# Attention, experts and a gated second stage on one core: weight sums earlier, token splits staggered, a third load buffer, conversions moved

## The chip, the cores and the metric

The kernel runs on one core of one Trainium2 chip. The metric is device microseconds (us) for one execution, compared as medians of several runs. Five engines work side by side and meet by semaphores: TensorE (PE; PEld is its weight load), VectorE (DVE), ScalarE (ACT), GpSimd (POOL) and SyncE (SP), which here issues nearly all DMAs. Each engine takes its instructions strictly in the order in which they were written for it.

## The reference, cut to what matters

```python
x = attention(q, k, v)                       # 4 batches, 8 heads, 768 positions, 64 wide
x = x.reshape(3072, 512)
x = x + gate * (relu(x @ w1[e]) @ w2[e])     # for kept tokens; e = best of 8 experts; w1 512x1024, w2 1024x512
gate = 1 / (1 + exp(-(x @ w_gate)))          # second stage: w_gate, w_val 512x1536
val = x @ w_val
return (gate * val) @ w_out                  # w_out 1536x512
```

The inputs of the second stage's weights come as 8-byte floats, which the kernel turns into 4-byte ones itself.

## The kernel before, in words

**Order.** Attention with the routing comes first (to about 290 us), then the experts 1 to 7 (290 to 493 us) and one tile of overflow tokens (493 to 508 us), then the second stage (508 us to the end).

**Experts.** Each expert takes 256 tokens. Its first products are four groups (`hook1` is called after each), its second products four more (`hook2`). `hook2` splits the next expert's w1 into a high and a low part, one of four chunks at a call (`split_chunk`: ACT copies the high part, L798; DVE subtracts, L799). Both hooks also advance the conversions of the second stage's weights: `CSE[e]` says how many half conversions each of the eight calls makes. One conversion is a load by SP (`cv_load`, tile `cvw`, 512 KB), a square on ACT (L1359), five DVE operations (L1372 to L1379), an addition on POOL (L1380), and a store from ACT's queue (`cv_store`). 28 of the 36 conversions (`NCE`) are made in the experts, eight in the second stage, two half ones in each of its first steps. Loads run two conversions ahead in the experts and one ahead in the second stage.

**Second stage.** Tokens come in three groups of 1024, and each group makes twelve steps. A step (`first_product`) is a 2x2 matrix product in the form with seven products instead of eight. One side needs seven combinations of the four token blocks (`xsplit`, tiles `B11`, `B21`, `B22`, `B1` to `B4`), the other the four weight blocks and four sums of them (`wsums`, tile `ws`, four POOL additions, L1140 to L1143). Every operand is split into a high and a low part; a product is six matmuls of 128x512 (L1222). `wsplit(s, 0)` splits the weights themselves, `wsplit(s, 1)` the sums (L1149 on ACT, L1150 on DVE). DVE adds the products up (L1228); a step ends in sigmoids or in gate times value, and half of the hidden values go to DRAM (`hd`) and come back later.

**Items.** The output product is cut into items of 12 matmuls each (L1189). An item's weights are loaded four items ahead (`item_load`, tile `wo`, with `hf` for the hidden values that come back), and split two items ahead (`item_split`: ACT L1171 and L1178, DVE or POOL L1172, DVE L1179). From step 2 on, each step carries one item in between its products. After the twelfth step of the first and the second group, twelve items run alone, and among them lies the change to the next group's tokens: at the third and the seventh of the twelve, PE turns the tokens of one half (`turn`, L1095) into the four banks of PSUM that the products use too, and `xsplit` works through them, one piece after each quarter of an item. `xsplit` for half 0 subtracts the low parts of its combinations on POOL, for half 1 on DVE (L1107).

**Entry to the second stage.** SP issues `load_w(0)`, `load_w(1)` and the token loads at the end of the experts. The order written out at the start of the second stage is: `wsums(0)` on POOL, both `wsplit` of step 0, `load_w(2)`, `wsums(1)`, both turns, both `xsplit` interleaved, loads and splits of the first items, then the steps. There are four banks for turned tokens and products together (`ps_a`), so a product needs the bank of a piece that `xsplit` has read for the last time.

Of the kernel before, what the change touches and what calls it, by code (L numbers as in the profile page):

```python
# [9 lines left out]
F32 = mybir.dt.float32  # L10
F32R = mybir.dt.float32r
I32 = mybir.dt.int32
U32 = mybir.dt.uint32
AF = mybir.ActivationFunctionType
ALU = mybir.AluOpType
# [3 lines left out]
P = 128  # L19
# [4 lines left out]
DM = H * D  # L24
# [28 lines left out]
NSTEP = NGR * NM  # L53
# [2 lines left out]
FAR = BIG * 2.0 ** H  # L56
WT1, WT2, WT3 = 2, 3, 3
NCE = 28
C7 = 1, 1, 1, 1, 1, 1, 1, 2
CSE = (None, (0, 0, 1, 1, 0, 1, 1, 1), C7, C7, C7, C7, C7, (1, 1, 1, 1, 1, 1, 0, 0))  # L60


def _i32(c):
# [4 lines left out]
def attention_moe_glu_kernel(  # L68
# [7 lines left out]
    nc = tc.nc  # L76
    n_global, n_local, g_gate, g_val, g_out = [a.bitcast(I32) for a in (n_global, n_local, g_gate, g_val, g_out)]
    cp = ctx.enter_context(tc.tile_pool(name="cp", bufs=1))
# [40 lines left out]
    raw_p = wctx.enter_context(tc.tile_pool(name="raw_p", bufs=2))  # L119
# [637 lines left out]
    def cv_load(n):  # L757
        if n < 3 * NM:
            cvw[n] = load_words(nc, cvp, f"g{n}", cv_src(n)[0])
# [4 lines left out]
        wr = cvw.pop(n)  # L764
        return convert(nc, cvp, f"g{n}", wr, squares(nc, cvp, f"g{n}", wr), cvt[n])

    wf = {}

    def load_w(s):
        if s < NSTEP:  # L770
            wf[s] = cvp.tile([P, 4, 2 * P], F32, tag="w", name=f"w{s}")
            nc.sync.dma_start(wf[s], wd[s % NM].rearrange("p m c f -> p m (c f)").rearrange(
                "p m (k e) -> p (m k) e", k=2))

    def cv_store(n):
        if n in cvt:
# [3 lines left out]
    with ExitStack() as ectx:  # L780
# [254 lines left out]
        run(conv)  # L1035
        load_w(0)
        load_w(1)

        x0 = [cvp.tile([P, 2, DM], F32, tag="cvw", name=f"xr0_{a}", bufs=4) for a in range(4)]

# [17 lines left out]
    with ExitStack() as gctx:  # L1058
# [12 lines left out]
        def tmp(tag, name, bufs=2):  # L1071
            return tm_p.tile([P, HT], F32, tag=tag, name=name, bufs=bufs)
# [27 lines left out]
        def xsplit(g, c, pt):  # L1100

            Bt = xB[g]

            def parts(k, src, eng):
                th = Bt[k][:, 0, c]
                A.activation(th, src, AF.Copy)  # L1106
                eng.tensor_tensor(Bt[k][:, 1, c], src, th.bitcast(F32), ALU.subtract)  # L1107

            E = (G, V)[c]
            tags = [("cp", 6)] * 5 if g == 0 and c else [("sg", 5)] * 5  # L1110
            t = [tmp(tag, f"t{g}_{c}_{k}", n) for k, (tag, n) in enumerate(tags)]
            A.activation(t[4], pt[0, 1], AF.Copy)
            parts("11", pt[0, 0], V)
            yield
            parts("21", pt[1, 0], V)
            yield
            V.tensor_tensor(t[0], t[4], pt[0, 0], ALU.subtract)
            yield
            V.tensor_tensor(t[1], pt[1, 1], t[0], ALU.subtract)  # L1119
            parts("2", t[1], E)  # L1120
            yield
            parts("1", t[0], E)
            yield
            V.tensor_tensor(t[2], pt[1, 1], t[4], ALU.subtract)  # L1124
            parts("3", t[2], E)
            yield
            V.tensor_tensor(t[3], pt[1, 0], t[1], ALU.subtract)
            parts("4", t[3], E)
            yield
            parts("22", pt[1, 1], V)  # L1130
            yield


        ws, wsp = {}, {}

        def wsums(s):
            if s < NSTEP:
                w = wf[s]
                t = ws[s] = tm_p.tile([P, 4, 2 * P], F32, tag="ws", name=f"ws{s}", bufs=1)
                G.tensor_tensor(t[:, 0], w[:, 2], w[:, 3], ALU.add)  # L1140
                G.tensor_tensor(t[:, 1], t[:, 0], w[:, 0], ALU.subtract)
                G.tensor_tensor(t[:, 2], w[:, 0], w[:, 2], ALU.subtract)
                G.tensor_tensor(t[:, 3], w[:, 1], t[:, 1], ALU.subtract)  # L1143

        def wsplit(s, i):
            if s < NSTEP:
# [10 lines left out]
        def item_load(n):  # L1157
            if n < len(items):
                g, h, m = items[n]
                wof[n] = tmp("wo", f"wo{n}")  # L1160
                nc.sync.dma_start(wof[n], od[m])
                if h:
                    hf[n] = tmp("hf", f"hf{n}")
                    nc.sync.dma_start(hf[n], hd[m])

        def item_split(n):
            if n < len(items):
                g, h, m = items[n]
                t = wos[n] = (tm_p if n % 3 == 2 else raw_p).tile([P, 2, DM], F32R, tag="raw", name=f"wos{n}", bufs=1 if n % 3 == 2 else 2)
                src = wof.pop(n)  # L1170
                A.activation(t[:, 0], src, AF.Copy)  # L1171
                (V if h else G).tensor_tensor(t[:, 1], src, t[:, 0].bitcast(F32), ALU.subtract)  # L1172
                if h:
                    hidden_split(g, h, m, hf.pop(n))
# [98 lines left out]

        def conversions():
            for n in range(NCE, 3 * NM):
                if n == NCE:
                    cv_load(n)
                cv_load(n + 1)
                it = cv_steps(n)
                next(it)  # L1280
                yield
                next(it)
                cv_store(n - 1)
                yield
            cv_store(3 * NM - 1)
# [1 line left out]
        conv = conversions()  # L1287


        wsums(0)  # L1290
        wsplit(0, 0)
        wsplit(0, 1)
        load_w(2)
# [8 lines left out]
        for n in range(4):  # L1302
            if n > 1:
                item_split(n - 2)
            item_load(n)
        n = 0
        for s in range(NSTEP):
            g, pk = divmod(s, NM)
# [508 lines left out]
```

## Time and profile before

| | us |
|---|---|
| median of 3 runs (lowest, highest) | 1125.66 (1125.36, 1126.01) |
| the profiled execution's own time | 1127.95 |
| its span, first to last instruction | 1126.2 |
| PE busy in the span | 1050.3 (93%) |
| DVE busy in the span | 832.0 (74%) |

The span is what the rows divide up. PE is busy nearly throughout, so the places to look for are those where PE waits, and what released it there; the timeline names the releaser in brackets behind an instruction.

### The profile page before, as it was taken

The numbers are of one execution on the slowest core, as the hardware profiler recorded it, in microseconds if no ns is written. First come the engines' busy times: TensorE is split into PE (matmuls) and PEld (weight loads), VectorE is DVE, ScalarE is ACT, GpSimd is POOL, SyncE is SP. The second block draws the span as 40 slices with busy tenths as digits, with TensorE's granted clock in tenths as the row PEclk, the third lists the DMA queues.
The fourth block names the chain that finished last, engine by engine and source line by source line (L and its number), as shares of the span: only waits on it lengthen the run. The fifth ranks groups of instructions, "written<-read, shape, count | busy, mean of one in ns | idle before, by whom it ended". The sixth has DMA issues, their size and how long they took to land. (4 is left out here: it accounts for less than half of the span.)

```text
span 1126.2 us, 16867 instructions
## 1 busy us (share of the span) xinstructions
PE 1050.3 (93%) x5602; PEld 853.4 (76%) x5602; DVE 832.0 (74%) x1693; ACT 531.1 (47%) x963; POOL 487.9 (43%) x523
## 2 busy tenths in 40 slices
PE   7999999998999898995698999989999989999998
PEld 7999999886776675754566678778888868888886
DVE  6778888874666878846688887757777775877653
ACT  5897878751333333334233334444344454343333
POOL 6665656551324343335355564114555311555410
PEclk8999999988999999997899999999999999999999
DMA  9565555523988888841333343533224444323144
GB/s 176 123 167 130 134 128 135 161 68 97 381 298 289 307 292 313 307 162 57 111 131 131 113 159 103 180 101 134 81 78 166 138 143 117 107 85 95 65 150 150
DMA packets 156387, 176.37 MB, mean 157 GB/s; under 512 B 84224, under 2 KB 106496, under 8 KB 156288
## 3 DMA queue, kind: packets, MB, share of 16 engines
q1 hardware_dynamic: 148384, 156.81, 45.1%
q10 hardware_dynamic: 5184, 9.44, 2.2%
q0 software_dynamic: 2720, 8.92, 2.1%
q8 instruction: 48, 0.79, 0.3%
q14 instruction: 51, 0.42, 0.1%
HBM read 133.45 MB, written 36.18 MB: 151 GB/s over the span
## 5 line engine op out<-in xcount | busy, mean ns | idle before, releaser
L1222 PE MATMUL p<-B,wsp 128*128 128x512 f32 x1512 | 373.4, 397 | 29.7 <-DVE cp L1228 14.7
L1222 PEld LDWEIGHTS p<-B,wsp 128*128 128x128 f32 x1512 | 286.3, 191 | 100.8 <-issue 24.1
L1189 PE MATMUL o<-wos,gt 128*128 128x512 f32 x864 | 220.6, 395 | 11.5 <-ACT gt L1178 7.4
L1228 DVE TENSOR_TENSOR cp<-p,cp 128x512 f32<-128x512 f32 x252 | 167.6, 684 | 75.3 <-PE p L1222 69.4
L1189 PEld LDWEIGHTS o<-wos,gt 128*128 128x128 f32 x864 | 162.3, 189 | 51.1 <-ACT gt L1178 9.7
L1172 POOL TENSOR_TENSOR wos<-wo,wos 128x512 fp32r<-128x512 f32 x36 | 61.3, 1704 | 110.1 <-ACT wos L1171 110.1
L401 ACT ACTIVATE p<-t,mn 128x256 f32<-128x256 f32 (+1 forms) x192 | 83.6, 485 | 38.7 <-DVE mn L392 38.1
L857 PE MATMUL y<-raw,hT 128*128 128x512 f32 x224 | 99.6, 592 | 0.0
L1235 ACT ACTIVATE sg<-cp 128x512 f32<-128x512 f32 x72 | 45.1, 632 | 114.9 <-DVE cp L1228 114.3
L1178 ACT ACTIVATE gt<-gm 128x512 fp32r<-128x512 f32 x36 | 22.8, 632 | 155.4 <-DVE gm L1242 155.4
L838 PE MATMUL h<-xeh,we 128*128 128x256 f32 x448 | 88.3, 297 | 7.5 <-DVE we L799 7.5
L1140 POOL TENSOR_TENSOR ws<-w 128x256 f32<-128x256 f32 x36 | 26.5, 737 | 153.3 <-DVE wsp L1150 144.8
L1380 POOL TENSOR_TENSOR cvd<-cvd,cvbg 128x512 f32<-128x512 f32 x36 | 58.1, 1620 | 64.3 <-issue 35.6
L392 DVE CUSTOM_DVE_ANT_0 t<-s,far 128x256 f32<-128x256 f32 (+1 forms) x192 | 69.0, 397 | 19.7 <-PE s L367 15.8
L279 POOL TENSOR_TENSOR ks<-ring,ks 128x384 fp32r<-128x384 f32 x56 | 56.2, 1024 | 60.6 <-DVE ks L278 52.3
L838 PEld LDWEIGHTS h<-xeh,we 128*128 128x128 f32 x448 | 72.7, 198 | 10.1 <-DVE we L799 8.2
L367 PE MATMUL s<-ks,qs 128*128 128x256 f32 (+1 forms) x384 | 70.5, 303 | 5.3 <-POOL ks L279 2.7
L857 PEld LDWEIGHTS y<-raw,hT 128*128 128x128 f32 x224 | 41.0, 190 | 43.6 <-issue 43.3
L439 PE MATMUL o<-v,pts 128*128 128x65 f32 x384 | 70.6, 276 | 0.0
L1238 POOL TENSOR_TENSOR gm<-cp,sg 128x512 f32<-128x512 f32 x36 | 53.4, 1483 | 30.3 <-DVE cp L1228 30.3
L838 PE MATMUL h<-xel,we 128*128 128x256 f32 x224 | 64.7, 289 | 0.0
L1150 DVE TENSOR_TENSOR wsp<-w,wsp 128x1024 fp32r<-128x1024 f32 x36 | 58.8, 1632 | 7.2 <-ACT wsp L1149 6.7
(276 smaller groups left out, 1932.4 us busy)
## 6 DMA issues: line engine op xcount, KB each, us to landing
raw<-in_moe_w_dram SPq DMA_DIRECT2D x68, 512.0 KB
w<-wd SPq DMA_DIRECT2D x36, 512.0 KB
wo<-od SPq DMA_DIRECT2D x72, 256.0 KB
hd<-gm SPq DMA_DIRECT2D x36, 256.0 KB
hf<-hd SPq DMA_DIRECT2D x36, 256.0 KB
qraw<-in_q_dram SPq DMA_DIRECT2D x32, 192.0 KB
kraw<-in_k_dram SPq DMA_DIRECT2D x32, 192.0 KB
v<-in_v_dram SPq DMA_DIRECT2D x8, 768.0 KB
```

The source lines that it names most:

```text
L367: nc.tensor.matmul(st[:, a, c0:256], qt[:, a, i * P:(i + 1) * P], kt[:, a, e, k0:(i + 1) * P], start=(e == 0), stop=(e == 1))
L392: nc.vector.tensor_tensor_reduce(o, i0, i1, 2.0 ** -(h0 + 1), 3.0e38, ALU.add, ALU.min, mn[:, a:a + 1])
L401: nc.scalar.activation(p[:, a, c0:], t[:, a, c0:], AF.Exp, bias=mn[:, a:a + 1], scale=-1.0)
L439: nc.tensor.matmul(o[:, hh, :], t[:, a, 1, :], vt[:, hh, i, :], start=(i == 0), stop=True)
L838: nc.tensor.matmul(ph[:, a, :n], chunks[cb + c][:, wl, m * P:(m + 1) * P], xx[:, c, :n], start=(s_ == 0), stop=(s_ == len(seq) - 1))
L857: nc.tensor.matmul(ys[u], hh[:, f % 2, u * P:(u + 1) * P], w[:, (f % 2) * DM:(f % 2 + 1) * DM], start=(f == 0), stop=(f == NF - 1))
L1150: V.tensor_tensor(t[:, 1], src, t[:, 0].bitcast(F32), ALU.subtract)
L1172: (V if h else G).tensor_tensor(t[:, 1], src, t[:, 0].bitcast(F32), ALU.subtract)
L1189: nc.tensor.matmul(o[u], gt[:, hl, u * P:(u + 1) * P], w[:, wl, :], start=(m == 0 and i == 0), stop=(m == NM - 1 and i == 2))
L1222: nc.tensor.matmul(ps, w[:, wl, q, c * P:(c + 1) * P], Bt[k][:, xl, c], start=i == 0, stop=i == len(seq) - 1)
L1228: V.tensor_tensor(into, ps, t, ALU.add)
L1380: nc.gpsimd.tensor_tensor(dst, dst, b, ALU.add)
```

## The change

Four things change. The four POOL additions of `wsums(0)` are written at the end of the experts' stage (tile `ws` moves to a pool that lives there). `xsplit` makes the same operations in five pieces instead of eight, with the low parts a piece behind the high ones, and the four differences sooner. `wo` and `hf` have three buffers instead of two (a third `raw` tile is taken from another pool for it). The conversions are counted out anew: more of an expert's half conversions after its first products, fewer among its second ones, none in the last expert's second products; in the second stage the first two loads are issued ahead of the steps, and later ones two ahead.

```diff
-C7 = 1, 1, 1, 1, 1, 1, 1, 2
-CSE = (None, (0, 0, 1, 1, 0, 1, 1, 1), C7, C7, C7, C7, C7, (1, 1, 1, 1, 1, 1, 0, 0))
+C7 = 2, 2, 1, 1, 0, 1, 1, 1
+CSE = (None, (0, 0, 1, 1, 0, 1, 1, 1), C7, C7, C7, C7, C7, (2, 2, 1, 1, 0, 0, 0, 0))
...
         load_w(0)
         load_w(1)
+        wsums(0)
...
             E = (G, V)[c]
+            src = {"11": pt[0, 0], "21": pt[1, 0], "22": pt[1, 1], "1": t[0], "2": t[1], "3": t[2], "4": t[3]}
+            sub = lambda o, x, y: V.tensor_tensor(o, x, y, ALU.subtract)
+            high("11")
             A.activation(t[4], pt[0, 1], AF.Copy)
-            parts("11", pt[0, 0], V)
+            high("21")
+            low(V, "11")
+            sub(t[0], t[4], pt[0, 0])
             yield
-            parts("21", pt[1, 0], V)
+            sub(t[1], pt[1, 1], t[0])
+            low(V, "21")
+            high("22")
             yield
-            V.tensor_tensor(t[0], t[4], pt[0, 0], ALU.subtract)
+            high("2", "1")
+            sub(t[2], pt[1, 1], t[4])
+            sub(t[3], pt[1, 0], t[1])
             yield
-            V.tensor_tensor(t[1], pt[1, 1], t[0], ALU.subtract)
-            parts("2", t[1], E)
+            low(E, "2", "1")
+            high("3", "4")
+            low(V, "22")
             yield
-            parts("1", t[0], E)
+            low(E, "3", "4")
             yield
-            ... (t[2], "3"; t[3], "4"; "22": three more pieces)
...
-                wof[n] = tmp("wo", f"wo{n}")
+                wof[n] = tmp("wo", f"wo{n}", 3)
...
-                    hf[n] = tmp("hf", f"hf{n}")
+                    hf[n] = tmp("hf", f"hf{n}", 3)
...
-                if n == NCE:
-                    cv_load(n)
-                cv_load(n + 1)
+                cv_load(n + 2)
...
-        wsums(0)
         wsplit(0, 0)
         wsplit(0, 1)
...
             item_load(n)
+        cv_load(NCE)
+        cv_load(NCE + 1)
```

(`parts` was the copy of a high part on ACT followed at once by the subtraction of the low part.)

## Rows read from the trace of the kernel before

**Rows 1.** Windows: length, busy us (x instructions) by engine, PE clock, DMA share, GB/s.
```profile
290.00:508.00 218.00, 210.05 (x1036) 144.98 (x1035) 157.72 (x220) 72.33 (x105) 82.50 (x60) 0.98 0.81 290
508.00:545.00 37.00, 18.92 (x76) 13.97 (x77) 23.15 (x29) 15.68 (x25) 15.75 (x15) 0.77 0.28 93
...
698.00:744.00 46.00, 40.46 (x181) 31.73 (x180) 34.04 (x47) 23.70 (x43) 9.17 (x7) 0.96 0.47 155
744.00:891.00 147.00, 147.00 (x650) 121.66 (x649) 106.60 (x132) 59.12 (x85) 69.82 (x71) 1.00 0.33 110
891.00:935.00 44.00, 38.53 (x176) 29.96 (x176) 32.23 (x46) 23.32 (x43) 8.45 (x6) 1.00 0.49 157
```
**Rows 2.** Timeline of PE, entry to second stage: start, us, count [idle before <-releaser].
```profile
508.72 3.69 PE L1095 MATMUL gx<-ident,xr 128*128 128x128 f32 x32 [1.10 <-DVEq L1735]
...
528.52 2.90 PE L1222 MATMUL p<-B,wsp 128*128 128x512 f32 x6 [6.63 <-DVE t L1127]
...
544.25 11.88 PE L1222 MATMUL p<-B,wsp 128*128 128x512 f32 x42 [6.82 <-DVE cp L1228]
```
**Rows 3.** Timelines of POOL, ACT, DVE and SP at the same entry.
```profile
508.69 2.02 POOL L912 DMA_INDIRECT x_rows<-xo,idx  x1 [12.04 <-DVEq L1735]
...
501.52 1.06 ACT L1149 ACTIVATE wsp<-w 128x1024 fp32r<-128x1024 f32 x1 [0.41 <-ACTq L1735]
513.67 1.06 ACT L1149 ACTIVATE wsp<-ws 128x1024 fp32r<-128x1024 f32 x1 [11.09 <-POOL ws L1143]
...
508.64 1.23 DVE L1150 TENSOR_TENSOR wsp<-w,wsp 128x1024 fp32r<-128x1024 f32 x1 [0.23 <-DVEq L1735]
515.90 2.69 DVE L1107 TENSOR_TENSOR B<-gx,B 128x512 fp32r<-128x512 f32 x4
...
541.54 0.43 DVE L1372 TENSOR_SCALAR cvd<-cvwg 128x512 int32<-128x512 int32 x1 [6.10 <-DMA cvwg<-in_moe_w_out_dram]
...
514.34 19.77 SPq L1161 DMA_DIRECT2D wo<-od  x4
...
535.28 0.86 SPq L1352 DMA_DIRECT2D cvwg<-in_moe_w_out_dram  x2
```
**Rows 4.** Groups by line, 508 to 545 us: xcount | busy us, mean ns | idle.
```profile
L1107 POOL TENSOR_TENSOR B<-t,B 128x512 fp32r<-128x512 f32 x4 | 5.5, 1386 | 5.9 <-ACT B L1106 5.9
L1107 DVE TENSOR_TENSOR B<-t,B 128x512 fp32r<-128x512 f32 x4 | 5.5, 1388 | 2.1 <-ACT B L1106 2.1
...
L1107 DVE TENSOR_TENSOR B<-gx,B 128x512 fp32r<-128x512 f32 x6 | 3.8, 682 | 0.1
```
**Rows 5.** Timeline of PE and DVE at the two changes of group.
```profile
716.18 2.60 PE L1189 MATMUL o<-wos,gt 128*128 128x512 f32 x10 [1.18 <-DVE gt L1179]
...
720.28 8.93 PE L1189 MATMUL o<-wos,gt 128*128 128x512 f32 x36
730.17 3.45 PE L1189 MATMUL o<-wos,gt 128*128 128x512 f32 x12 [0.96 <-ACT gt L1178]
736.44 7.42 PE L1189 MATMUL o<-wos,gt 128*128 128x512 f32 x24 [2.82 <-ACT gt L1178]
...
928.75 6.29 PE L1189 MATMUL o<-wos,gt 128*128 128x512 f32 x24 [2.80 <-ACT gt L1178]
...
714.37 1.75 DVE L1179 TENSOR_TENSOR gt<-hf,gt 128x512 fp32r<-128x512 f32 x1
```
**Rows 6.** Waits of SP, 676 to 746 us: total us, times, longest.
```profile
SPq L1161 <- DVE wos L1172: 23.9, 10, 5.4
```
**Rows 7.** The chain of waits at the first change of group: start, us.
```profile
720.58 2.79 DMA wo<-od
```
**Rows 8.** Waits, 280 to 510 us: total us, times, longest.
```profile
PE h L838 <- DVE we L799: 7.5, 3, 3.5
```
**Rows 9.** Timelines of SP and DVE inside the third expert.
```profile
355.86 2.04 SPq L1350 DMA_DIRECT2D cvwg<-in_moe_w_gate_dram  x2
...
367.18 1.89 DVE L1372 TENSOR_SCALAR cvd<-cvwg 128x512 int32<-128x512 int32 x1 [4.90 <-DMA cvwg<-in_moe_w_gate_dram]
```

More of the change, by code (lines that the diff above doesn't have):

```diff
@@ L765, in cv_steps @@
         return convert(nc, cvp, f"g{n}", wr, squares(nc, cvp, f"g{n}", wr), cvt[n])
-    wf = {}
+    wf, ws = {}, {}
     def load_w(s):
@@ L773, in load_w, with wsums @@
                 "p m (k e) -> p (m k) e", k=2))
+    def wsums(s):
+        if s < NSTEP:
+            w = wf[s]
+            t = ws[s] = cvp.tile([P, 4, 2 * P], F32, tag="ws", name=f"ws{s}", bufs=1)
+            for k, (x, y, op) in enumerate(((w[:, 2], w[:, 3], ALU.add), (t[:, 0], w[:, 0], ALU.subtract),
+                                            (w[:, 0], w[:, 2], ALU.subtract), (w[:, 1], t[:, 1], ALU.subtract))):
+                nc.gpsimd.tensor_tensor(t[:, k], x, y, op)
     def cv_store(n):
@@ L1102, in xsplit, with high, low @@
             Bt = xB[g]
[L1104 to L1107, printed above, removed]
+            tag, n = ("cp", 6) if g == 0 and c else ("sg", 5)
+            t = [tmp(tag, f"t{g}_{c}_{k}", n) for k in range(5)]
+            def high(*keys):
+                for k in keys:
+                    A.activation(Bt[k][:, 0, c], src[k], AF.Copy)
+            def low(eng, *keys):
+                for k in keys:
+                    eng.tensor_tensor(Bt[k][:, 1, c], src[k], Bt[k][:, 0, c].bitcast(F32), ALU.subtract)
@@ L1109, in xsplit @@
             E = (G, V)[c]
-            tags = [("cp", 6)] * 5 if g == 0 and c else [("sg", 5)] * 5
-            t = [tmp(tag, f"t{g}_{c}_{k}", n) for k, (tag, n) in enumerate(tags)]
+            src = {"11": pt[0, 0], "21": pt[1, 0], "22": pt[1, 1], "1": t[0], "2": t[1], "3": t[2], "4": t[3]}
+            sub = lambda o, x, y: V.tensor_tensor(o, x, y, ALU.subtract)
+            high("11")
             A.activation(t[4], pt[0, 1], AF.Copy)
-            parts("11", pt[0, 0], V)
+            high("21")
@@ L1121, in xsplit @@
+            high("3", "4")
+            low(V, "22")
             yield
-            parts("1", t[0], E)
+            low(E, "3", "4")
             yield
[L1124 to L1143, printed above, removed]
+        wsp = {}
@@ L1168, in item_split @@
                 g, h, m = items[n]
-                t = wos[n] = (tm_p if n % 3 == 2 else raw_p).tile([P, 2, DM], F32R, tag="raw", name=f"wos{n}", bufs=1 if n % 3 == 2 else 2)
+                t = wos[n] = xa.tile([P, 2, DM], F32R, tag="xT", name=f"wos{n}") if n % 3 == 2 else raw_p.tile([P, 2, DM], F32R, tag="raw", name=f"wos{n}")
                 src = wof.pop(n)
```

## The prediction, made before the changed kernel ran

> **What bounds the kernel now.** I read the windows by stage first. From 744 to 891 us PE is busy all 147.00 us with 650 instructions at full clock: 0.226 us a matmul, nothing to win there. The reader is to see the other stretches beside it: 508 to 545 us, where PE is busy 18.92 of 37.00 us and its granted clock averages 0.77 (between its two levels, 1.2 and 2.4 GHz), and the two changes of group, 698 to 744 and 891 to 935 us [rows 1]. At 0.226 us a matmul and 3.69/32 = 0.115 us a transposition, the change from 698 needs 149 x 0.226 + 32 x 0.115 = 37.4 us and takes 46.0, an excess of 8.6; the one from 891 needs 144 x 0.226 + 3.7 = 36.2 and takes 44.0, an excess of 7.8 [rows 1, 2]. Then the timelines say what PE waited for: in the entry 6.63 us for DVE's differences of tokens and 6.82 us for a DVE addition [rows 2], at the changes three kinds of waits for split operands [rows 5]. In the experts the waits of PE for DVE's weight splits come to 7.5 us [rows 8]. So PE sets the end, and what can be won is its waiting: about 18 us in the entry, 16 in the changes, 7.5 in the experts.
>
> **Part 1, the entry (weight sums, stagger, early conversion loads): 13 us.** Before, POOL stood idle 12.04 us, issued a scatter at 508.69 (2.02 us) and only then made the four sums, until 513.67: 2.96 us of work. ACT stood for 11.09 us on them, and behind it in ACT's order stood the first copies of tokens; DVE began the token split at 515.90 [rows 3]. Written ahead, the sums lie in POOL's 12.04 us. Their wait is for the weights' load, which was there when ACT copied the same weights at 501.52; behind them on POOL stands only that scatter. Without that cover they would cost 2.96 us again. DVE then goes on from 508.64 + 1.23 with the second weight split, another 1.2: done at 511.1, 4.8 us ahead of 515.90.
>
> What is late next is DVE's own work: per half seven operations on PSUM, in all 14 at 2.69/4 = 0.67 us, 9.4 us [rows 3], and four low parts of half 1 at 0.69 to 1.39 us, 2.8 to 5.6 us; the 2.1 us that it waited for ACT's copies are gone, for a copy now has a piece's time to finish (the lower end by the PSUM row, 0.68) [rows 4]. It ends at 523.3 to 526.1. Four high and low pairs of half 0 on POOL change their order and not their number.
>
> Then the conversion. DVE's first one stood 6.10 us, to 541.54, for a load that SP issued at 535.28, since SP was held until 514.34 + 19.77 = 534.1 by the third and fourth `wo` loads, which waited for the two buffers [rows 3]. Now the third has its own buffer. The fourth waits for the first item's split on POOL, which comes after the second sums (511.1 + 2.96 = 514.1) and four low parts at 1.39, so to about 520, and as much again for the split: 521.4. The conversion loads go out at about 522; issue to use was 541.54 - 535.28 = 6.26 us, so they land at 528.3. DVE gets there at 526 to 529 (an addition, a weight split, an addition: 0.68 + 1.23 + 0.68 = 2.6 us after the token split). PE went on 544.25 - 541.54 = 2.7 us after the conversion's start [rows 2, 3]: now 531.0 to 531.8. PE itself: seven products from about 512.4; at 2.7 us each, twice 6 x 0.226, as at the half clock (528.52: 2.90 for six), 18.9 us, also 531. Three chains end together, so I take 531.2 for 544.25: 13 us. Bounds: 4.8 (only the sums' lead counts, the load stays as late against DVE), and 15 (DVE at 523.3 + 2.6 + 2.7 = 528.6, the load in time). The eight steps that follow are set by DVE's conversions, whose number is unchanged: nothing.
>
> **Part 2, the changes of group (third buffers, stagger): 6.5 and 5.5 us.** SP waited 23.9 us in 676 to 746 for DVE's splits of `wo`, ten times [rows 6]: a load four items ahead took the buffer of the split just written, so it left late and its 2.79 us stood in the chain, `wo` landing just before ACT's copy [rows 7]. With three buffers it takes the buffer of the split an item earlier, 2.72 us sooner, about its own length: it leaves the chain. What is late next is DVE. One item takes PE 12 x 0.226 = 2.72 us; DVE has two splits for it, 1.35 us at 0.68, and for half 1 the seven and the four operations, 11 x 0.67 = 7.4 us, mostly within two items. Two items' slack (5.4 us) and 1.37 us spare per item cover that. So after the second turning (720.28) six items follow at 16.3 us, 736.6 instead of 743.86: 7.2 us, of which 0.96 + 2.82 are waits, 7.42 - 24 x 0.226 = 2.0 is the half clock behind them, and the rest stretched matmuls [rows 5]. In the first half of the change I leave the 1.18 us wait as it is and take off 0.7 for DVE work that now comes in one lump: 6.5. The second change has the same rows (2.80 for 2.82, but 6.29 for 7.42): 5.5. Bounds of the two: nothing, and the whole excess, 8.6 and 7.8.
>
> A rule weighed here. DVE's 1.75 us for `gt` at 714.37, and 1.388 us a low part, fall where POOL subtracts low parts at 1.386; a low part of the same size with its source in PSUM took 0.68 [rows 4, 5]. The Trainium skill (SBUF — State Buffer, "SBUF: two separate sides") says that a DVE operation with two SBUF inputs and a GpSimd one exclude each other for a whole instruction; the trace agrees, with 1.388 and 1.386. That speaks against the stagger: POOL's four low parts of half 0 now come packed.
>
> Worked out from rows: the fourth item waits for two DVE splits, and before only one of them met POOL (1.75 for 0.68, 1.07 lost). If both meet a packed POOL, each is held for up to a whole 1.39, 2.8 us in all, 1.7 more than before at each change: Part 2 is 12 - 3.4 = 8.6 by that alone.
>
> **Part 3, conversions in the experts: 3 us.** Number and length are unchanged (nine half ones an expert, six in the last); six instead of four stand before the second products and their weight splits, and two instead of three between the first split and the last. Before, a load issued at 355.86 was waited for until 367.18, 11.3 us, with the DMA engines at 0.81 and 290 GB/s [rows 1, 9]; DVE then did conversions and splits on top of each other and PE stood up to 3.5 us [rows 8]. One half conversion less ahead of the last split is up to 2.0 us of DVE (2.7 from 541.54 to PE's restart, less an addition of 0.68) at each of two such boundaries; 3 us of the possible 4, since the loads are no faster. Bounds: 7.5 gained, and 5 lost (one new stop of 1 us in each of five experts).
>
> **Sum.** 13 + 12 + 3 = 28. The profiled execution took 1127.95 us, with 1.75 us around its span of 1126.2, and would take 1100; it was 2.3 above the median, so for medians I say 1125.66 - 28 = 1098.
>
> **The rivals.**
> - *The load takes over the entry* (17%). SP is still held by the fourth `wo` load, behind a POOL split in a queue with DVE's differences; if that split comes at 527 rather than 521.4, the conversion starts near 534.5 and Part 1 is 7: 1104. For it: SP's 19.77 us; against it: the third load waits for nothing.
> - *DVE stays late through the changes* (15%). POOL's packed low parts take the 1.7 us above, and DVE, with 1.35 + 3.7 us an item in the two items of half 1 against PE's 2.72, doesn't make it up before PE gets there: the 2.82 us wait and its 2.0 us of half clock stay at the first change, 2.8 at the second. Part 2 is 12 - 3.4 - 4.8 - 2.8 = 1: 1109. For it: 1.388 for 0.68; against it: DVE's 1.37 us to spare in each item between the halves.
> - *All waits go* (8%): experts 7.5, both changes their whole excess with 16.4, entry 15: 39, 1087.
> - *Slower* (3%). In an expert whole conversions now follow the first and second of eight calls, so the next conversion's load has about a quarter of an expert between issue and use: 218/8 = 27 us, so 7 us, against 11.3 measured [rows 1, 9]. ACT's square waits for it, and behind it in ACT's order stand the copies of hidden values that PE's second products read. DVE's 4.90 us wait cost PE nothing on the spot, so that much slack I grant. To undo 25 us and lose 2.3, five experts must lose 5.5 each: the load lands 7 + 4.9 + 5.5 = 17.4 us after issue, and from there on it is 1128 and up. Against it: nothing in the rows comes near 17.
> - *It does not bind* (2%): PE's waits reappear elsewhere, 1124 to 1128.
>
> **How the numbers follow.** The forecast has 55%, with 1092 to 1103 as its own range. With the first two rivals and half of the third the range is 1089 to 1110. About 0.2% is what a measurement of this kernel can tell from no change: faster 0.95, same 0.02, slower 0.03.
>
> **What would show it.** Sums: ACT's second weight copy before 505, DVE's token split from about 511. Loads: DVE's wait for the first conversion under 2.5 us, PE's second step near 531. Changes: SP's waits for DVE splits of `wo` near nothing, PE's waits of 0.9 and 2.8 gone after the second turning, the first of 1.2 still there. Experts: PE's waits for weight splits between 3 and 5 us. It is wrong if the second step still starts after 537, or if the changes keep over 6 us of excess each.

## The result, and the profile after

The changed kernel took 1111.23 us, median of 4 runs (1107.65 to 1112.28); the kernel before took 1125.84 beside it (4 runs, 1125.36 to 1128.83). The ratio is 0.9859, 95% interval [0.9831, 0.9887]: faster, by 14.6 us where 28 were forecast. The median is 1.2 us above the upper end of the range; by the ratio, on the 1125.66 that the forecast started from, it is 1109.8, just inside. The profiled execution of after took 1112.28 with a span of 1110.6, against 1126.2.

I cut both profiled executions at the same four marks of PE: the first transposition of the hidden values of expert 0's second tile (`ht0b`, just ahead of experts 1 to 7), the first turning of tokens into the second stage, the 43rd product matmul behind it (PE's second step), and for each change of group its first turning and the next first-stage product. The profile after by those stages (windows; length, busy us (x instructions) of PE, PEld, DVE, ACT and POOL, PE clock, DMA share, GB/s), to be held against [rows 1]:

```profile
290.00:511.00 221.00, 211.52 (x1042) 146.25 (x1040) 161.19 (x222) 72.31 (x107) 84.71 (x64) 0.98 0.81 287
...
512.00:538.00 26.00, 18.13 (x74) 11.66 (x72) 20.66 (x27) 14.51 (x24) 13.91 (x11) 0.87 0.41 145
692.00:732.00 40.00, 37.99 (x182) 31.14 (x181) 33.82 (x48) 23.15 (x43) 10.11 (x8) 1.00 0.57 186
878.00:919.00 41.00, 38.97 (x180) 31.77 (x179) 33.87 (x48) 23.15 (x43) 10.07 (x8) 0.96 0.55 180
```

| stage, by marks of PE (us) | before | after | gained | forecast |
|---|---|---|---|---|
| start to `ht0b` | 288.58 | 289.55 | -1.0 | 0 |
| experts: `ht0b` to first turning | 220.14 | 222.24 | -2.1 | 3 |
| entry: first turning to second step | 35.53 | 26.66 | 8.9 | 13 |
| first change: turning to next first-stage product | 39.92 | 33.61 | 6.3 | 6.5 |
| second change, the same | 38.82 | 35.19 | 3.6 | 5.5 |

The first line is not the change's: over the 14 profiled executions of this study, with the same work in that stretch, this mark lies between 283.70 and 289.55.

**Entry.** PE's timeline (start, us, count, in brackets the idle time before and its releaser), against [rows 2]:

```profile
511.79 3.46 PE L1105 MATMUL gx<-ident,xr 128*128 128x128 f32 x30 [1.10 <-DVEq L1740]
...
519.30 1.95 PE L1228 MATMUL p<-B,wsp 128*128 128x512 f32 x3 [3.13 <-ACT B L1118]
...
538.45 3.88 PE L1228 MATMUL p<-B,wsp 128*128 128x512 f32 x9 [2.19 <-DVE cp L1234]
```

The wait of 6.63 us has gone and the one of 6.82 is down to 2.19; a new one of 3.13 us, for ACT's copy of a token tile, stands near the front, and shorter ones (0.67, 1.54 and 0.56 us) lie between the last two of these lines. The other engines in the same stretch of after (POOL, ACT, DVE and SP timelines), against [rows 3]:

```profile
511.76 2.03 POOL L921 DMA_INDIRECT x_rows<-xo,idx  x1 [9.09 <-DVEq L1740]
...
505.62 1.04 ACT L1155 ACTIVATE wsp<-ws 128x1024 fp32r<-128x1024 f32 x1
518.16 1.08 ACT L1118 ACTIVATE B<-gx 128x512 fp32r<-128x512 f32 x2 [3.96 <-DMA x_rows<-xo,idx]
...
513.99 0.68 DVE L1122 TENSOR_TENSOR B<-gx,B 128x512 fp32r<-128x512 f32 x1
519.28 0.69 DVE L1122 TENSOR_TENSOR B<-gx,B 128x512 fp32r<-128x512 f32 x1 [4.01 <-ACT B L1118]
535.75 0.43 DVE L1377 TENSOR_SCALAR cvd<-cvwg 128x512 int32<-128x512 int32 x1 [1.18 <-DMA cvwg<-in_moe_w_out_dram]
...
513.69 17.86 SPq L1167 DMA_DIRECT2D wo<-od  x4
```

ACT copies the sums at 505.62 instead of 513.67, and DVE begins the token split 2.2 us behind the first turning instead of 7.2. Then ACT stands 3.96 us until the overflow tile's scatter (`x_rows<-xo`) has landed: the second token tile lies in memory that `xo`, the scatter's source, has just given up (e3 below tests this). DVE waits 4.01 us behind ACT. The conversion's wait for its load is 1.18 us, down from 6.10.

**Changes of group.** PE's timeline of after at the first and the second change, against [rows 5]:

```profile
708.86 1.08 PE L1195 MATMUL o<-wos,gt 128*128 128x512 f32 x2 [0.75 <-ACT gt L1184]
711.12 2.57 PE L1195 MATMUL o<-wos,gt 128*128 128x512 f32 x10 [1.19 <-DVE gt L1185]
...
715.20 16.61 PE L1195 MATMUL o<-wos,gt 128*128 128x512 f32 x72
...
894.86 1.07 PE L1195 MATMUL o<-wos,gt 128*128 128x512 f32 x2 [0.77 <-ACT gt L1184]
897.11 4.15 PE L1195 MATMUL o<-wos,gt 128*128 128x512 f32 x10 [1.18 <-DVE gt L1185]
```

Behind the second turning six items run without a wait (at the second change too, from 902.76). In the first half the stops stay, and in the second change the ten matmuls behind them take 4.15 us instead of 2.57, at the lower clock. This loss comes and goes with the same instructions: six profiled executions have the changes as in after (after, e1, e2, e3, e5, e7), and of their twelve changes three take 33.6 to 33.7 us at a granted clock of 1.00 and nine take 35.1 to 35.3 at 0.95. So 6.3 us at the first change is the rarer outcome; the commoner one would have been 4.7. SP still waits for buffers, 17.9 us where it was 23.9 [rows 6] (waits of SP in after, 660 to 740 us: total, times, longest):

```profile
SPq L1167 <- DVE wos L1178: 17.9, 9, 6.0
```

**Experts.** PE's waits for weight splits grew from 7.5 us [rows 8] to (after, 280 to 515 us):

```profile
PE h L847 <- DVE we L808: 9.1, 3, 3.4
```

Where they come from shows in the timelines of POOL, ACT and DVE of after inside an expert:

```profile
330.45 1.00 POOL L861 DMA_INDIRECT x_rows<-xo,idx  x1 [2.75 <-DVE xo L860]
338.50 1.24 POOL L861 DMA_INDIRECT x_rows<-xo,idx  x1 [7.05 <-DVE cvd L1377]
339.77 2.49 POOL L1385 TENSOR_TENSOR cvd<-cvd,cvbg 128x512 f32<-128x512 f32 x2
...
341.50 0.69 ACT L1364 ACTIVATE cvcg<-cvwg 128x512 f32<-128x512 f32 x1 [8.24 <-POOL cvd L1385]
...
331.19 0.69 DVE L1384 SCALAR_TENSOR_TENSOR cvbg<-cvwg,cvbg 128x512 f32<-128x512 uint32 x1
```

POOL's queue stands some 7 us before the second scatter of an expert, until 0.8 us after the first one has landed (337.70); the addition whose input DVE had finished at 331.88 starts at 339.77, the first of the two there; the store of that conversion stands ahead of ACT's next square, which stops for 8.24 us. So the experts carry a wait that the prediction didn't name.

### The profile page after: what moved, and what is told of

The parts are those of the page before. It is cut to its first block, busy times and chain, and to the rows that moved or that the text cites. A ratio compares the mean times of both kernels' runs of the same rounds, so it can differ in the third digit from the quotient of the medians.

```text
span 1110.6 us, 16877 instructions
## 1 busy us (share of the span) xinstructions
PE 1046.9 (94%) x5602; PEld 852.3 (77%) x5602; DVE 832.7 (75%) x1693; ACT 527.8 (48%) x963; POOL 489.5 (44%) x523
## 5 line engine op out<-in xcount | busy, mean ns | idle before, releaser
L1228 PE MATMUL p<-B,wsp 128*128 128x512 f32 x1512 | 373.6, 396 | 21.2 <-DVE cp L1234 12.4
L1195 PE MATMUL o<-wos,gt 128*128 128x512 f32 x864 | 217.7, 393 | 4.5 <-DVE gt L1185 2.4
L782 POOL TENSOR_TENSOR ws<-w 128x256 f32<-128x256 f32 x72 | 54.6, 758 | 146.2 <-DVE wsp L1156 146.2
L1385 POOL TENSOR_TENSOR cvd<-cvd,cvbg 128x512 f32<-128x512 f32 x36 | 55.3, 1545 | 64.2 <-issue 30.6
```

The lines of the kernel that those rows point to most:

```text
L1195: nc.tensor.matmul(o[u], gt[:, hl, u * P:(u + 1) * P], w[:, wl, :], start=(m == 0 and i == 0), stop=(m == NM - 1 and i == 2))
L1228: nc.tensor.matmul(ps, w[:, wl, q, c * P:(c + 1) * P], Bt[k][:, xl, c], start=i == 0, stop=i == len(seq) - 1)
```

## The experiments

Each row of this table is cut at the same marks. "Ratio" is against the kernel before on the same chip, with its 95% interval; all kernels but the last change the kernel after.

| kernel | median | ratio | experts | entry | changes |
|---|---|---|---|---|---|
| before | 1125.84 | | 220.14 | 35.53 | 39.92, 38.82 |
| after | 1111.23 | 0.9859 [0.9831, 0.9887] | 222.24 | 26.66 | 33.61, 35.19 |
| e1, old count | 1108.21 | 0.9827 [0.9795, 0.9860] | 220.02 | 26.42 | 35.11, 35.14 |
| e2, store later | 1119.13 | 0.9948 [0.9898, 0.9998] | 231.01 | 25.98 | 35.25, 35.19 |
| e3, tile order | 1108.74 | 0.9843 [0.9805, 0.9882] | 225.31 | 22.16 | 35.27, 33.62 |
| e4, pieces slower | 1103.80 | 0.9804 [0.9767, 0.9840] | 221.52 | 26.60 | 31.73, 31.71 |
| e5, addition on DVE | 1100.60 | 0.9767 [0.9730, 0.9805] | 213.85 | 26.17 | 35.06, 35.16 |
| e6, three edits | 1101.71 | 0.9784 [0.9747, 0.9821] | 223.98 | 21.31 | 31.80, 31.70 |
| e7, halves behind the splits | 1121.68 | 0.9954 [0.9923, 0.9986] | 234.04 | 26.07 | 33.72, 35.12 |
| e8, two buffers | 1110.24 | 0.9851 [0.9811, 0.9891] | 222.15 | 27.71 | 34.54, 34.36 |
| e9, eight pieces | 1117.69 | 0.9933 [0.9909, 0.9956] | 220.63 | 30.17 | 36.51, 38.07 |
| e10, four edits | 1087.98 | 0.9658 [0.9635, 0.9681] | 213.08 | 21.57 | 31.60, 31.66 |
| e11, four edits, old count | 1086.84 | 0.9650 [0.9627, 0.9673] | 213.18 | 21.56 | 31.67, 31.68 |
| e12, before, addition on DVE | 1117.44 | 0.9937 [0.9915, 0.9959] | 210.43 | 34.54 | 41.13, 39.94 |

The stages come from one execution each. Six executions with the same edit state in the experts (after, e3, e4, e6, e8, e9) spread from 220.6 to 225.3 there, so a single figure of that column is good to some 2 us; in the last column the lower clock alone moves a figure by 1.6.

### The count of conversions in the experts (e1, e7)

e1 takes the old count back:

```diff
-C7 = 2, 2, 1, 1, 0, 1, 1, 1
-CSE = (None, (0, 0, 1, 1, 0, 1, 1, 1), C7, C7, C7, C7, C7, (2, 2, 1, 1, 0, 0, 0, 0))
+C7 = 1, 1, 1, 1, 1, 1, 1, 2
+CSE = (None, (0, 0, 1, 1, 0, 1, 1, 1), C7, C7, C7, C7, C7, (1, 1, 1, 1, 1, 1, 0, 0))
```

> The changed kernel with the old count of half conversions in the experts (1,1,1,1,1,1,1,2); all else as changed. Theory: PE's stops for weight splits come from POOL, whose second scatter of an expert waits some 7 us for its first; a conversion's addition stands behind it on POOL, its store waits for that on ACT's queue, and the squares and splits stand behind the store. The count only chooses at which expert boundaries this shows: three stops of 9.1 us in all (new count) against 7.5 us in three (old count), so 1.5 us faster than the changed kernel or the same, 1109 to 1111 us. Rival (the prediction's step): fewer half conversions ahead of the last split are worth 3 us, so the old count is slower by 3, 1114 us.

It took 1108.21. PE's waits for weight splits are those of before again (e1, 280 to 515 us):

```profile
PE h L847 <- DVE we L808: 7.6, 3, 3.5
```

So the new count, for which I had counted 3 us gained, gains nothing and probably costs 2 to 3; the two ratios' intervals still overlap.

e7 goes further along the prediction's idea, fewer half conversions ahead of the last weight split:

```diff
-C7 = 2, 2, 1, 1, 0, 1, 1, 1
+C7 = 2, 2, 1, 1, 0, 0, 0, 3
```

> The changed kernel, with an expert's half conversions counted out as 2, 2, 1, 1, 0, 0, 0, 3 instead of 2, 2, 1, 1, 0, 1, 1, 1: none stands between the first and the last weight split, three stand behind the last. Theory 2 (half conversions between the splits make the last split late): PE's waits for weight splits fall from 9.1 to under 3 us, 1105 us. Theory 1 (POOL's scatter holds everything): the conversions that follow the first two products are held as before, the splits start late all the same, and waits stay at 6 to 9 us; 1109 to 1112 us.

It took 1121.68, 10 us more than after. The waits for splits nearly went, and something else came (waits of PE and of ACT in e7, 280 to 515 and 285 to 500 us):

```profile
PE h L847 <- ACT hT L851: 17.6, 2, 9.0
PE h L847 <- DVE we L808: 1.3, 2, 0.7
...
ACT cvcg L1364 <- DMA cvwg<-in_moe_w_gate_dram: 36.8, 4, 12.5
```

With three halves at one call ACT's square waits up to 12.5 us for the next conversion's load, and the copies of hidden values stand behind it in ACT's order: the mechanism that the prediction held for its slower rival, in a count denser than the one changed. So with no half conversion between them the splits were hardly late, and the time was lost elsewhere.

### What holds the experts (e2, e5, e12)

e2 takes ACT's store out of the way of POOL's held addition, by writing it one conversion later:

```diff
-                cv_store(n - 1)
+                cv_store(n - 2)
...
+            cv_store(NCE - 2)
             cv_store(NCE - 1)
```

> The changed kernel, with a conversion's store in the experts written one conversion later in ACT's order, so that ACT seldom waits for POOL's addition. Theory (POOL's scatter holds ACT through the store): ACT's waits for the POOL addition L1385, 23.4 + 17.5 us, fall below 10, PE's waits for weight splits fall from 9.1 us to under 3, and the time by 5 to 7 us, to 1104 to 1106 us. Rival (late conversion loads hold DVE and ACT): those waits are replaced by waits for the loads, PE's stay near 9, 1111 us.

A miss: 1119.13, slower than after. ACT's waits for POOL's additions fell from 41 to 1 us, and the hold moved on (waits of PE and DVE in e2, 280 to 515 us):

```profile
PE h L847 <- DVE we L808: 14.7, 8, 3.5
...
DVE cvd L1378 <- DMA wd<-cvd: 24.7, 6, 5.9
```

A store that leaves a conversion later frees its buffer (there are three) later, and DVE, which splits the weights too, waits there instead of ACT.

e5 gives the addition to DVE, in the experts alone:

```diff
-    nc.gpsimd.tensor_tensor(dst, dst, b, ALU.add)
+    add.tensor_tensor(dst, dst, b, ALU.add)      # DVE for n < NCE, else POOL
```

> The changed kernel, with the last addition of a conversion (L1385) made by DVE instead of POOL in the experts. Theory 1: PE's stops there come from POOL: its second scatter of an expert waits some 7 us, the addition behind it holds store, buffer, square and split. Then DVE's and ACT's waits for stores and for POOL go, and PE's waits for weight splits fall from 9 us to under 4: 5 us faster than the changed kernel, 1106 us. Theory 2: DVE itself is too full around the splits (157.9 of 203 us busy in 290 to 493 before the addition); 28 x 0.7 = 20 us more on it, less what POOL's additions cost it by the shared port (28 x 1 us), changes little, stops of 7 to 11 us stay, 1109 to 1113 us.

It took 1100.60, 10.6 us under after; the experts' stage went from 222.24 to 213.85 us and PE's waits for weight splits in it from 9.1 to 4.2. The price that I had thought of, 28 additions more on DVE, doesn't appear. DVE and POOL by line in the experts, after (290 to 511 us: xcount | busy us, mean ns | idle before):

```profile
L1377 DVE TENSOR_SCALAR cvd<-cvwg 128x512 int32<-128x512 int32 x28 | 27.3, 974 | 18.9 <-DMA cvwg<-in_moe_w_gate_dram 11.0 <-DMA cvwg<-in_moe_w_val_dram 5.0 <-DMA od<-cvd 1.6
L1378 DVE SCALAR_TENSOR_TENSOR cvd<-cvwg,cvd 128x512 int32<-128x512 int32 x28 | 23.2, 830 | 1.0
...
L1385 POOL TENSOR_TENSOR cvd<-cvd,cvbg 128x512 f32<-128x512 f32 x28 | 43.3, 1557 | 64.2 <-issue 30.6 <-DVE cvbg L1384 27.0 <-DMA x_rows<-xo,idx 6.5
```

and e5 (287 to 500 us):

```profile
L1379 DVE SCALAR_TENSOR_TENSOR cvd<-cvwg,cvd 128x512 int32<-128x512 int32 x28 | 19.4, 693 | 1.0
L1386 DVE TENSOR_TENSOR cvd<-cvd,cvbg 128x512 f32<-128x512 f32 x28 | 19.4, 693 | 1.0
...
L1378 DVE TENSOR_SCALAR cvd<-cvwg 128x512 int32<-128x512 int32 x28 | 12.1, 434 | 16.7 <-DMA cvwg<-in_moe_w_gate_dram 10.3 <-DMA cvwg<-in_moe_w_val_dram 6.3
```

The 28 additions take DVE 19.4 us, and its other operations give nearly all of it back: the first operation of a conversion (L1377 in after, L1378 in e5) took 27.3 us and takes 12.1 and the second 23.2 and 19.4: 19.0 less. DVE's busy time in the two windows is 161.19 us with 222 instructions in after and 160.50 with 250 in e5. So the additions on POOL had cost DVE their own length all along. Single rows of after show how (timelines of POOL and DVE):

```profile
325.50 2.20 POOL L1385 TENSOR_TENSOR cvd<-cvd,cvbg 128x512 f32<-128x512 f32 x1 [8.29 <-DVE cvbg L1384]
...
326.47 1.51 DVE L1377 TENSOR_SCALAR cvd<-cvwg 128x512 int32<-128x512 int32 x1
```

DVE's operation ends at 327.98, 0.28 us behind POOL's addition. So it is with all twelve of the 28 that took over 0.8 us: each ends 0.28 to 0.30 us behind an addition. The Trainium skill (SBUF — State Buffer, "SBUF: two separate sides") has a rule for it: some DVE operations and a GpSimd one lock each other out for a whole instruction. The trace agrees, with these ends and with a mean of 974 ns beside POOL's 1557 and 434 without.

e12 makes the same edit on the kernel before.

> The kernel before with one edit: in the expert stage the addition that ends a conversion half is done by DVE instead of POOL (from the first conversion behind the experts on, by POOL as before). Theory: POOL's second scatter of an expert holds the additions queued behind it for some 7 us in the kernel before just as in the changed one, where DVE gave 10.6 us (median) and 8.4 us of the expert stage; the stage before takes 220.1 us against 222.2, so 5 to 8 us are to be had: 1117 to 1121. Rival (the hold is made by the new count of conversions, which bunches two halves in the first steps of an expert, right behind the scatters): no gain or a loss, 1124 to 1130, since DVE only gets more to do.

It took 1117.44, 8.4 us under the kernel before: the loss was there before the change, and the count doesn't make it. PE's waits in e12, 280 to 520 us:

```profile
PE h L839 <- DVE we L800: 1.7, 1, 1.7
```

and its window over the experts:

```profile
287.00:496.00 209.00, 206.73 (x1039) 142.10 (x1037) 160.28 (x249) 72.90 (x106) 37.31 (x32) 1.00 0.85 303
```

The waits fell by 5.8 us, and PE's busy time to 206.7 at a granted clock of 1.00, from 211.00 at 0.98 in before's stretch from 289 to 508 us (a little more than the first of [rows 1]): besides the waits, the stops had cost PE some 3.5 us of lower clock (4.3 us less busy, of which four instructions fewer are 0.8). Whether the scatter's hold of POOL's queue or the time that the additions take from DVE is the larger part isn't told apart: e5 removes both, and e2 removed only ACT's share of the hold.

### The entry (e3)

The order of the seven token tiles in memory is changed, so that the second one no longer lies where the scatter reads:

```diff
-  for k in ("11", "21", "22", "1", "2", "3", "4")}
+  for k in ("11", "4", "21", "22", "1", "2", "3")}
```

> The changed kernel, with the seven token tiles placed in another order in memory (11, 4, 21, ... instead of 11, 21, 22, ...), so that the tile which lies where the overflow tile's result xo lay is the one that is written last (4). Theory: ACT's 3.96 us wait in the entry, put down to the scatter of xo, is for that memory: the copy of 21 may not overwrite xo before the scatter has read it. Then the wait goes, DVE's token split ends 4 us sooner, SP's fourth load and the conversion loads behind it too: 3.5 to 4.5 us faster than the changed kernel, about 1107 us. Rival 1: the wait is for the turned tokens or a load, and stays: 1111 us. Rival 2: the wait goes, but the conversion load, not moved, takes its place: under 1.5 us.

It took 1108.74, which its interval doesn't tell from after (its experts, untouched, ran 3.1 us longer in the profiled execution). The entry itself fell from 26.66 to 22.16 us. ACT and PE at that place in e3 (timelines):

```profile
515.85 1.10 ACT L1118 ACTIVATE B<-gx 128x512 fp32r<-128x512 f32 x2
...
535.71 1.63 PE L1228 MATMUL p<-B,wsp 128*128 128x512 f32 x6 [1.72 <-DVE cp L1234]
```

ACT copies without a stop. That is 22.2 us behind the turning; the prediction's 531.2 was 22.5 behind it.

### The changes of group (e4, e8, e9)

e8 takes the third buffers back, and leaves the stagger:

```diff
-                wof[n] = tmp("wo", f"wo{n}", 3)
+                wof[n] = tmp("wo", f"wo{n}")
...
-                    hf[n] = tmp("hf", f"hf{n}", 3)
+                    hf[n] = tmp("hf", f"hf{n}")
```

> The changed kernel with two buffers again for the items' weights and hidden values. Theory (the prediction's): the third buffer carries most of Part 2; SP's waits for DVE's splits come back (about 24 us in the first change), the waits of 0.9 and 2.8 us after the second turning come back in part, and the changes lose 3 to 5 us each: 1118 to 1121 us; in the entry the third load waits for a split again, which costs nothing more than the fourth does already. Rival: the stagger carries it; ACT and DVE reach the splits in time even with two buffers, and the time stays at 1111 to 1113 us.

It took 1110.24, the same as after. SP waits more (e8, waits of SP, 660 to 740 us):

```profile
SPq L1167 <- DVE wos L1178: 19.8, 10, 6.0
SPq L1167 <- POOL wos L1178: 13.4, 3, 8.2
```

and PE hardly notices; its only new stop behind the second turning is (e8, PE's timeline; 0.16 us at the second change):

```profile
722.41 8.64 PE L1195 MATMUL o<-wos,gt 128*128 128x512 f32 x35 [0.15 <-DVE wos L1178]
```

e9 does the reverse: the old split in eight pieces (high and low part of a tile together, the low parts of `22` last), with three buffers and the rest of the change.

```diff
-            high("21")
-            low(V, "11")
-            sub(t[0], t[4], pt[0, 0])
+            parts("11", pt[0, 0], V)
             yield
-            sub(t[1], pt[1, 1], t[0])
-            low(V, "21")
-            high("22")
+            parts("21", pt[1, 0], V)
             yield
...
```

> The changed kernel with the token split back in eight pieces (each high part followed by the low part that reads it, as before the change); three buffers, early weight sums, early conversion loads and the new count stay. Theory 1 (the stagger carries the changes of group; the buffers, taken back alone, gave 1110.24 against 1111.23): the subtraction again stands behind the copy that it reads and the last token sums come later, so PE stops again in the products between the turns, and the changes lose most of the 6.3 + 3.6 us that they gained and the entry loses some of its 8.9 too: 1118 to 1125. Rival (the lead grew for another reason: the loads and the weight sums come earlier and would carry it in either order): within 3 us of the changed kernel, 1108 to 1114.

It took 1117.69. PE in e9, entry and the two changes (timeline):

```profile
526.02 2.90 PE L1223 MATMUL p<-B,wsp 128*128 128x512 f32 x6 [6.29 <-DVE t L1137]
...
727.93 6.29 PE L1190 MATMUL o<-wos,gt 128*128 128x512 f32 x24 [2.27 <-ACT gt L1179]
...
916.70 7.91 PE L1190 MATMUL o<-wos,gt 128*128 128x512 f32 x24 [2.28 <-ACT gt L1179]
```

With three buffers the first wait behind the second turning (0.96, [rows 5]) is gone and the last is 2.27 for 2.82; the changes take 36.51 and 38.07 (24 matmuls in 7.91 us at the second, 6.29 at the first). So by themselves the buffers are worth 3.4 and 0.8 us there, the stagger (e8) 5.4 and 4.5, both 6.3 and 3.6: with the stagger in place, the buffers add less than a microsecond to the first change, and nothing to the median. Part of these differences is the clock behind a stop, which fell in some of the changes and not in others. Changes without that loss (a granted clock of 1.00) take 38.8 us in before, 36.5 in e9, 34.4 and 34.5 in e8 and 33.6 in after: compared so, the buffers alone are worth 2.3 us a change, the stagger alone 4.3 to 4.5, both 5.2. At the entry the stagger is 3.5 of the 8.9 us (30.17 to 26.66).

e4 lets the pieces of a token split come after every second quarter of an item instead of every one:

```diff
-                    for _ in item(n):
-                        for it in turning:
+                    for u, _ in enumerate(item(n)):
+                        for it in turning if u % 2 == 0 else ():
```

> The changed kernel, with the pieces of the token split at the two changes of group taken after every second quarter of an item instead of every quarter. Theory: the stop in the first half of each change (0.75 + 1.19 us, and at the second change about 1.6 us of half clock behind it) comes from DVE and ACT doing the token pieces in one lump ahead of the next item's splits; spread out, the stops fall below 1 us at each change and the time by 2 to 5 us, 1106 to 1109 us. Rival: the stop is fixed by when SP can issue the loads of that item behind the hidden values' stores and by the shared port between POOL and DVE; then it stays, 1111 us. If the second half's pieces come too late for the first product, a new wait for token tiles appears there instead.

It took 1103.80. Both changes take 31.7 us, and of the stops in the first half none is left, only a short one behind the second turning (PE in e4, timeline):

```profile
707.98 0.71 PE L1195 MATMUL o<-wos,gt 128*128 128x512 f32 x2
709.15 3.01 PE L1195 MATMUL o<-wos,gt 128*128 128x512 f32 x12 [0.46 <-DVE gt L1185]
```

DVE and POOL at the stop in after (timelines, first change):

```profile
706.29 5.92 POOL L1122 TENSOR_TENSOR B<-t,B 128x512 fp32r<-128x512 f32 x4 [8.87 <-ACT B L1118]
...
709.30 1.76 DVE L1185 TENSOR_TENSOR gt<-hf,gt 128x512 fp32r<-128x512 f32 x1
710.99 1.77 DVE L1178 TENSOR_TENSOR wos<-wo,wos 128x512 fp32r<-128x512 f32 x1
712.69 0.68 DVE L1185 TENSOR_TENSOR gt<-hf,gt 128x512 fp32r<-128x512 f32 x1
```

Two splits take 1.76 and 1.77 us beside POOL's packed low parts and 0.68 when POOL is done. In e4 two splits still take 1.80 and 1.77 beside POOL (705.61 and 707.33), but with the pieces further apart PE doesn't meet them. That the slowed splits made the stops of after, and not the token pieces in one lump by themselves, is argued from these rows; e4 changes the second and leaves the first.

### The parts together (e6, e10, e11)

e6 joins e3 and e4 and issues the first two conversion loads ahead of the items' loads (`cv_load(NCE)`, `cv_load(NCE + 1)` moved above the loop over `item_load`).

> The changed kernel with three edits together, each in its own stretch: the other order of the token tiles in memory (4.5 us gained in the entry by its trace), token pieces after every second quarter (about 7 us over both changes of group), and the first two conversion loads of the second stage issued ahead of the loads of the items instead of behind them. Theory: the parts add up, and the third takes away DVE's remaining 1.2 us wait for the first conversion and what the load would hold of the earlier split: from the turn of the tokens to PE's second step 20 us instead of 26.7, and 1098 to 1100 us in all. Rival: the entry is then held by PE at half clock or by DVE, the third edit gives nothing: 1101 us.

It took 1101.71, above the 1098 to 1100 expected: entry 21.31, changes 31.8 and 31.7, each as in the single runs, but for 0.85 us off e3's entry, which goes with the loads: in e3 the first conversion waits 0.72 us for its load, in e6 not at all. e10 adds e5's edit.

> Four edits together on the changed kernel: conversion additions of the experts on DVE (alone 1100.60, that is 10.6 us under the changed kernel), the tile order with 4 behind 11 (alone 2.5 us), pieces of the token split after every second quarter at the changes (alone 7.4 us), the first two conversion loads ahead of the weight loads. If the stops of the experts, of the entry and of the changes are separate, the parts add: the three without the addition gave 1101.71, the addition takes 10 more, 1090 to 1094. Rival (the DVE that adds is late at the entry, so that the weight split there ends later and eats the gain): 1097 to 1102.

It took 1087.98, lower than the forecast of 1090 to 1094: the stages are those of the parts, 213.08, 21.57, 31.60 and 31.66. POOL's second scatter still waits as long, with no addition of a conversion queued behind it (e10, timeline):

```profile
335.87 1.04 POOL L862 DMA_INDIRECT x_rows<-xo,idx  x1 [7.02 <-DMA x_rows<-xo,idx]
```

Here the releaser is named: the first scatter into the same DRAM tensor has to land first.

e11 is e10 with the old count of e1.

> The same four edits with the old count of conversions by step (one in each of seven steps of an expert, two in the last, and one in each of the first six steps of the last expert). The old count alone gave 1108.21 against 1111.23. If it is worth its 3 us by itself: 1087 to 1091, 3 under the kernel with the new count. Rival: the old count helped only by spreading POOL's additions past the scatters, and with the additions on DVE there is nothing left for it to give: within 1.5 us of that kernel, or above it, since DVE then has an addition in steps where it splits weights.

It took 1086.84, its interval on top of e10's, and the experts are alike, 213.18 and 213.08: with the additions on DVE the count no longer matters. Either kernel is faster than before and after: by the medians e10 takes 2.1% less than after.

## Why the prediction was right and where it failed

**Faster, by half.** The direction rested on PE's waits being on the path that sets the end, and that held: the gains of the four stages and the -1.0 at the start sum to 15.7 us, and the spans differ by 15.6. The size failed in three terms of the sum.

**Part 1, 13 us, was 8.9.** The sums' lead came as worked out, 5 us by DVE's begin against the turning; so did the load's wait (1.18 us, under the 2.5 named), though SP was held until 531.55, where 521.4 was forecast. The step that failed is "the 2.1 us that it waited for ACT's copies are gone": the sums had hidden another release. In before ACT came to its first copies at 514.6, when the scatter issued at 508.69 had nearly landed (at about 514.9, an estimate from the 6.2 us that it takes in after); with ACT there at once, it waits 3.96 us for the scatter of the overflow tile to stop reading. Without that wait the entry is 22.2 us (e3) and the term right to 0.4 us. (The upper bound of this part comes to 15.6 us by the prediction's own terms, not 15; nothing hangs on it.)

**Part 2, 6.5 and 5.5, was 6.3 and 3.6: the sizes nearly, the reason not.** The prediction let the third buffer take the `wo` load out of the chain, and asked of the stagger only that it do no harm. e8 and e9 say that the stagger alone is worth 5.4 and 4.5 and leaves the third buffer next to nothing. Of the 1.9 us missing in the second change 1.6 are the ten matmuls at the lower clock (4.15 for 2.57); in the first change they ran at full clock. That the first came so near to 6.5 is luck, since nine of the twelve changes cut like this one lost those 1.6 us; 4.7 and 3.6 are the sizes to compare with 6.5 and 5.5. SP's waits didn't go "near nothing" (17.9), which cost nothing. The weighed rule did show up, in the first half of the change rather than the second: 1.76 and 1.77 us beside POOL, and e4 shows the stops there to be worth 5.4 us over both changes, the matmuls at the lower clock behind them included (7.4 us by the medians of e4 and of after).

**Part 3, 3 us, was -2.1.** The step that failed is "One half conversion less ahead of the last split is up to 2.0 us of DVE": the new count left the waits at 9.1 us where the old has 7.5 and 7.6. With none between the splits (e7) those waits do fall to 1.3 us, but the kernel is 10 us slower; e5 and e12 show what made the splits late in either count, POOL's additions, by the queue that its scatters hold and by the DVE time that they take. The prediction read [rows 9] as a late load; the same row has 1.89 us for an operation that takes 0.43 in [rows 3], and over the experts of before its mean is 1005 ns. Of the 12.4 us by which the sum of 28 missed the profiled 15.6, this term is 5.1, the entry 4.1, the second change 1.9, the first 0.2 and the start 1.0.

**The rivals.** "The load takes over the entry" came half: SP was held even past its 527, since the fourth item's split stood behind the late low parts on POOL; but DVE was late with them, and the load's own share is the 0.7 to 0.9 us by which e6 differs from e3. "DVE stays late through the changes" had the right mechanism in a place where it had cost 1.2 us before already; the waits behind the second turning went. "Slower" didn't happen in this count; e7 shows its place and price in a denser one.

## What to carry to other kernels

When a wait that is about to be removed stands at the head of an engine's queue, look for the next release it has been hiding, memory handed from one stage to the next included: a tile can wait for a DMA that only reads what lay there before. Compare an instruction's mean in each stage with its shortest form: where DVE's mean is twice that, another engine's work may be paid for on DVE, and moving that work to DVE can be free. Two changes of one execution with the same stops can differ by the clock behind them: compare stages at the same granted clock before crediting an edit. Two remedies for one wait don't add; test each alone before crediting either.

## What the runs showed of the hardware that was not expected

- DVE took on 28 additions, 19.4 us, and was busy 160.50 us where it had been 161.19 (e5 and after, experts): POOL's 28 additions of 1557 ns had held it for as much.
- The granted clock behind a stop of PE isn't told by the stop's length. After stops of 2.48 us (to 356.78) and of 3.12 us (to 472.30) in two experts of the changed kernel its windows read:

```profile
358.00:360.00 2.00, 2.00 (x12) 2.00 (x12) 1.97 (x4) 1.06 (x2) 1.85 (x2) 0.51 1.06 397
...
474.00:476.00 2.00, 2.00 (x19) 2.00 (x19) 1.85 (x4) 1.16 (x2) 1.72 (x2) 1.00 1.03 407
```

  Behind the shorter stop the clock was at about the lower of its two levels, 1.2 of 2.4 GHz, until 361.5; behind the longer one it stayed at the upper. The same pair of stops in the two changes of group (0.75 and 1.19 us, 0.77 and 1.18) cost 1.6 us of lower clock in the second and none in the first; over six executions it cost that in nine changes of twelve.
- Two scatters into the same DRAM tensor from POOL's queue: in the first of the seven experts the second waited 7.32 us in before, 7.05 in after and 7.02 in e10, each time until 0.8 us after the first had landed, and what is queued behind it on POOL waits too.
